# A long convolution by Fourier stages beside a feed-forward: the spectra buffers K and U turned from [frequency, channel] to [channel, frequency], and the ranks of the tasks set anew

## The chip, the core and the metric

The kernel runs on one core of a Trainium2 chip. The metric is device time in microseconds of one execution; less is better. A core has a matrix engine (PE, with a separate row PEld for its weight loads), three engines for elementwise work (DVE, ACT, POOL), and SP, whose queue issues the DMAs. On-chip memory is SBUF and, for matmul results, PSUM; both have 128 partitions.

## What is computed

```
x = A_u                                        # [1, 2048, 640] float32
g = sigmoid((x * gate_w).sum(-1))              # one gate per position
# state-space convolution: a kernel K[d, l] of 2048 taps for each of 640 channels
dt = exp(log_dt);  A = -exp(log_A_real) + 1j * A_imag
C  = (C_real + 1j * C_imag) * dt[:, None]
K  = 2 * einsum("dn,dnl->dl", C, exp((A * dt[:, None])[:, :, None] * arange(L))).real
a  = irfft(rfft(K, 2L) * rfft(u^T, 2L), 2L)[:, :, :L]^T + u * D_skip
b  = relu(x @ w1) @ w2                         # 640 -> 1728 -> 640
out = g * a + (1 - g) * b
```

## The kernel before

Three strands of work share the engines.

- **Feed-forward** (`feed_forward`): three passes over parts of the 1728 hidden columns (5, 5 and 4 tiles of 128), eight groups of 256 positions in each. Operands are split into a high and a low part, and three products stand for one. In the views its matmuls write the tile `pf`; `pf<-xx,w1…` is the first layer and `pf<-w2…` the second. It has few dependencies on the rest and fills PE wherever the other strands wait.
- **Generation of the taps** (`params`, `ssm`): decay rates to phases and magnitudes (ACT with sine and exponential tables, DVE with products), then small matmuls into `pk`, a DVE transpose into `kt`, and a store of the taps to DRAM (`kd`).
- **The convolution** (`conv`), for five blocks `i` of 128 channels. A 2048-point transform is made of two stages of small matmuls. All of its matmul results go through a ring of three PSUM tiles named `pc`, and its spectra live in an SBUF tile `ku` with a half K for the taps and a half U for the signal, two such tiles for the five blocks. A half holds, on each partition, 32 frequencies (or time residues) by 128 channels, with the channels innermost: `[128, 32, C]`. The steps of one block are:
  1. `stage1`, four tasks for taps (source `ck`) and four for the signal (source `xu`): matmuls with the table `tf` into `pc`, and for each task two DVE transposes of 32 by 32 blocks (`turn`) from `pc` into K or U: 16 transposes.
  2. `stage2`, eight tasks `j`: 16 matmuls with the table `tm` whose moving operand is one frequency of K and of U, `st['ku', i][r, :, g]`, 256 columns; then an ACT copy of one half of the result into K (`ku<-pc`), two DVE products (`kx<-pc,ku` and, in place, `ku<-pc,ku`) and two POOL additions (`ku<-ku,kx`). `whole(i, j)` is the part of K that they share. This is the complex product of the two spectra.
  3. `inv2`, two halves: 64 matmuls each with `tn`, moving operand `whole(...)[r, q, p]` of 128 columns, then two ACT copies back into U (`back`, 128x1024).
  4. `relay`, eight DVE transposes from U into K (`ku<-ku`).
  5. `inv1`, four tasks: matmuls with `tw`, moving operand four time residues of K, 512 columns, then ACT multiplies by the gate into `yo`, and the results are joined with the feed-forward's and stored.

The program lists a float32 matmul once and the trace shows it as two instructions: 640 of the program with `tm` are 1280 in the trace.

The order is decided while the kernel is built. Each piece of work is a task (`Plan.add`) with an engine, a queue, a duration in us, dependencies, and a rank; `Plan.run` walks through time by these durations and takes on each engine the ready task of lowest rank, then issues it. On the chip every engine runs its instructions in that order. The rank of task number `n` is the one in its `add` plus `MOVES.get(n, 0)`; `MOVES` is a dictionary with one entry of ±0.7, ±1.5 or ±3 for some hundreds of the more than 2400 tasks. `relay` has a variant by DMA (`RL`), which is not in use. Lines of the profile are mostly L346, the helper through which all instructions are issued, so groups are told apart by tile names.

Of the kernel before, what the change touches and what calls it, by code (L numbers as in the profile page):

```python
# [60 lines left out]
RL = 'dve'  # L61
# [64 lines left out]
class Ring:  # L126
# [8 lines left out]
MOVES = {  # L135
# [59 lines left out]
}  # L195


class Task:
    __slots__ = ('eng', 'q', 'dur', 'fn', 'deps', 'take', 'use', 'prio', 'mode', 'lag', 'end', 'kb', 'glue', 'port', 'n', 'late')


class Plan:

# [164 lines left out]
class Kernel:  # L368
# [850 lines left out]
    def conv(self, C=128):  # L1219
# [49 lines left out]
        self.late_loads.append(tf)  # L1269
        K, first, pes = {}, {}, {}  # L1270


        def stage1(kind, i, q, src):
            s_, ld = src
            b_ = tok('psc')
# [267 lines left out]
```

## Time and profile before

| | |
|---|---|
| runs | 656.8, 662.4 and 1206.32 us; median 662.4 us |
| profiled execution | span 659.1 us; the page gives no other time of it, and what lies around the span is not shown |
| PE | 627.4 us busy (95%), 8236 matmuls |
| DVE | 550.5 us busy (84%), 778 instructions |
| ACT | 401.8 us busy (61%) |
| POOL | 93.5 us busy (14%) |
| mean granted clock of PE | 0.991 |

The share of busy time is a mean over strands with different limits. The generation of taps lies at about 85 to 395 us and the convolution at about 400 to 645 us of the span; feed-forward matmuls lie between them from start to end. A busy PE is not PE at its peak, since matmuls overlap. A row of a group reads: line, engine, operation, output from inputs, shapes, count, then busy time in us, the mean length of one in ns, and the idle time before them with what ended it. A row of the table by stretches gives start and end in us, length, busy time of each engine with the count of instructions, then the granted PE clock, the share of the DMA engines and GB/s.

### The profile page before, as it was taken

The page shows a single profiled execution, that of the slowest core. Times are in us where ns is not written, and L with a number is a line of the kernel's source. Part 1 is how long each engine was busy: PE and PEld are TensorE (multiplying, and loading weights), DVE is VectorE, ACT ScalarE, POOL GpSimd, SP SyncE. Part 2 cuts the span into 40 slices and gives each one's busy share as a digit, 9 for nine tenths or more (in the row PEclk, how much of TensorE's full clock was granted, in tenths as well). Part 3 has the DMA queues.
Part 4 walks back from the last instruction along what each step waited for, and adds up shares of the span by engine and source line. Part 5 has one row for each costly group of instructions (what it writes and reads, how often), then busy time and mean ns, then how long its engine had stood idle before and what let it go on. Part 6 is the DMA issues. An engine that isn't in the chain of part 4 may idle for free. (4 is left out here: it accounts for less than half of the span.)

```text
span 659.1 us, 19189 instructions
## 1 busy us (share of the span) xinstructions
PE 627.4 (95%) x8236; PEld 505.4 (77%) x8236; DVE 550.5 (84%) x778; ACT 401.8 (61%) x603; POOL 93.5 (14%) x133
## 2 busy tenths in 40 slices
PE   7999989999999999999999999998999999879896
PEld 7999989898987988998898995755666446735576
DVE  4899859999999899898999976894999778888552
ACT  5476389999998988979889821222431533334521
POOL 0000000000000000000000000240600622424541
PEclk9999999999999999999999999999999999989999
DMA  9963854143445532542424159946056756363526
GB/s 265 318 220 145 239 189 152 59 153 131 131 133 178 206 129 75 186 148 77 178 97 139 56 174 260 274 153 141 3 198 205 192 145 154 108 184 75 159 64 144
DMA packets 76303, 102.79 MB, mean 156 GB/s; under 512 B 7610, under 2 KB 59450, under 8 KB 75963
## 3 DMA queue, kind: packets, MB, share of 16 engines
q1 hardware_dynamic: 76058, 101.16, 51.0%
q8 instruction: 65, 1.06, 0.7%
q10 hardware_dynamic: 160, 0.41, 0.2%
q14 instruction: 20, 0.16, 0.1%
HBM read 62.36 MB, written 39.19 MB: 154 GB/s over the span
## 5 line engine op out<-in xcount | busy, mean ns | idle before, releaser
L346 PE MATMUL pf<-xx,w1h 128*128 128x256 f32 (+1 forms) x760 | 185.5, 341 | 0.8 <-ACT q L346 0.4
L346 PEld LDWEIGHTS pf<-xx,w1h 128*128 128x128 f32 x760 | 124.8, 190 | 30.6 <-issue 16.2
L346 PE MATMUL pf<-xx,w1l 128*128 128x512 f32 (+1 forms) x340 | 116.0, 341 | 3.0 <-issue 3.0
L346 PE MATMUL pf<-w2h,hh 128*128 128x320 f32 x288 | 89.2, 314 | 0.1
L346 PE MATMUL pf<-w2l,hh 128*128 128x320 f32 x288 | 87.8, 309 | 0.0
L346 ACT COPY ku<-pc 128x512 f32<-128x512 f32 (+1 forms) x60 | 42.8, 732 | 71.2 <-PE pc L346 71.0
L346 DVE STREAM_TRANSPOSE ku<-pc 128x512 f32<-128x512 f32 x80 | 76.4, 1051 | 10.1 <-PE pc L346 10.0
L346 PE MATMUL pf<-w2h,hl 128*128 128x320 f32 x256 | 74.0, 315 | 0.0
L346 PEld LDWEIGHTS pf<-xx,w1l 128*128 128x128 f32 x340 | 64.5, 190 | 7.7 <-DVE w1l L346 0.2
L346 POOL TENSOR_TENSOR ku<-ku,kx 128x256 f32<-128x256 f32 x80 | 55.9, 734 | 81.1 <-PE pf L346 31.0
L346 POOL TENSOR_TENSOR kt<-kt,dsk 128x8 f32<-128x8 f32 x20 | 10.3, 516 | 382.0 <-DVE kt L346 370.8
L346 DVE TENSOR_TENSOR sc<-pg,sc 128x1024 f32<-128x1024 f32 x40 | 48.7, 1217 | 12.1 <-ACT sc L346 11.9
L346 PEld LDWEIGHTS pf<-w2h,hh 128*128 128x128 f32 x288 | 54.1, 188 | 4.9 <-issue 2.4
L346 DVE STREAM_TRANSPOSE ku<-ku 128x512 f32<-128x512 f32 x40 | 46.9, 1237 | 10.7 <-ACT ku L346 8.6
L346 PEld LDWEIGHTS pf<-w2l,hh 128*128 128x128 f32 x288 | 54.1, 188 | 0.8
L346 ACT ACT_TABLE_LOAD x42 | 53.9, 1283 | 0.8
L346 ACT CAST sc<-pg 128x1024 int32<-128x1024 f32 x40 | 40.5, 1012 | 19.0 <-PE pg L346 18.7
L346 PEld LDWEIGHTS pf<-w2h,hl 128*128 128x128 f32 x256 | 46.2, 188 | 7.5 <-issue 7.1
L346 DVE TENSOR_TENSOR mg<-mg,sc 128x1024 f32<-128x1024 f32 x40 | 48.9, 1223 | 1.8
L346 DVE TENSOR_TENSOR sc<-sc,me 128x1024 f32<-128x1024 f32 x40 | 48.6, 1216 | 0.0
L346 ACT ACTIVATE yo<-pc,gate 128x128 f32<-128x128 f32 x78 | 22.1, 373 | 39.3 <-DMA out_dram<-yo 18.7
L346 ACT ACTIVATE sc<-sc,half_pi 128x1024 f32<-128x1024 f32 x40 | 45.6, 1139 | 0.0
(168 smaller groups left out, 1255.2 us busy)
## 6 DMA issues: line engine op xcount, KB each, us to landing
xx<-xt SPq DMA_DIRECT2D x24, 640.0 KB, 5.3
xt<-xx SPq DMA_DIRECT2D x16, 640.0 KB, 6.6
part<-q SPq DMA_DIRECT2D x16, 640.0 KB, 2.9
q<-part SPq DMA_DIRECT2D x16, 640.0 KB, 4.8
ws<-in_B_w_dram SPq DMA_DIRECT2D x20, 320.0 KB, 5.2
kd<-kt SPq DMA_DIRECT2D x80, 64.0 KB, 1.7
ck<-kd SPq DMA_DIRECT2D x40, 128.0 KB, 2.9
xu<-in_A_u_dram SPq DMA_DIRECT2D x10, 512.0 KB, 7.5
```

The lines of the kernel that those rows point to most:

```text
L346: return lambda *a, **k: self._tc.keep_in_program_order(f(*a, **k))
```

## The change

K and U keep their size, but the 128 channels become the outer and the 32 frequencies the inner index: a helper view `(e g f)` with `f=1` puts 32 frequencies of one channel next to each other. The transposes of `stage1` and `relay` now write (and `relay` also reads) runs without gaps; everything that takes one frequency for all channels now steps by 32 elements, 128 bytes: the moving operands of `tm`, `tn` and `tw`, the outputs of the ACT copies, one input of both DVE products, the output of the one in place, and the POOL additions' `ku` operands. The tile `kx` stays as it was. The planner's duration of a `stage1` transpose goes from 1.0 to 0.68, that of a relay from 1.17 to 0.7; the other durations stay. `MOVES` is replaced as a whole: a function `moves()` gives ranks to families of tasks, among them many tasks outside the convolution. The numbers of instructions by engine, and of DMAs, do not change. The order does, on every engine.

```diff
-RL = 'dve'
...
-MOVES = {
-    2: 1.5, 21: -3, 26: 1.5, 31: -1.5, 48: 3, 52: -3, 62: -1.5, 75: -1.5, 76: -0.7, 84: -3, 94: -0.7, 108: 0.7,
...
+def moves():
+    r = {}
+    for v, s in (
+            (-3.11, "739-741"),
+            (-2.81, "2"),
...
+            (-2.19, "1341-1677/56 1732"),
...
+            (0.51, "1266-1281/5"),
...
+            (3.6, "1327"),
+    ):
+        for x in s.split():
+            a, _, step = x.partition('/')
+            a, _, b = a.partition('-')
+            for i in range(int(a), int(b or a) + 1, int(step or 1)):
+                r[i] = v
+    return r
+MOVES = moves()
...
+        def blocks(x, d0):
+            return x[:, :, d0:d0 + 16].rearrange("p g e f -> p e f g")
...
-                        st['ku', i] = self.pr.tile([128, 2, 32, C], F32, name="ku", bufs=2)
+                        t = self.pr.tile([128, 2, 32, C], F32, name="ku", bufs=2)
+                        st['ku', i] = t.rearrange("p k a b -> p k (a b)").rearrange("p k (e g f) -> p k g e f", g=32, f=1)
                         st['K', i], st['U', i] = st['ku', i][:, 0], st['ku', i][:, 1]
...
-                    V.transpose(out=st['K' if k else 'U', i][:, :, d].rearrange("p g d -> p d g"), in_=pv)
+                    V.transpose(out=blocks(st['K' if k else 'U', i], d0), in_=pv)
...
-            ts = [A('DVE', 's' + kind, 1.0, turn(h), [a], use=[b_, buf], rank=SKD if k else SUD)
+            ts = [A('DVE', 's' + kind, 0.68, turn(h), [a], use=[b_, buf], rank=SKD if k else SUD)
...
         def whole(i, j):
-            return st['K', i][:, 4 * j:4 * j + 4].rearrange("q (b p) c -> q b p c", b=2)
+            return st['K', i][:, 4 * j:4 * j + 4].rearrange("q (b p) e f -> q b p e f", b=2)
...
         def relay(i, r, dep):
...
-            d = slice(r * 16, r * 16 + 16)
-            return A('DVE', 'rl', 1.17, lambda: V.transpose(out=st['K', i][:, :, d].rearrange("p b d -> p d b"),
-                                                           in_=st['U', i][:, :, d].rearrange("p g d -> p d g")),
+            return A('DVE', 'rl', 0.7, lambda: V.transpose(out=blocks(st['K', i], r * 16), in_=blocks(st['U', i], r * 16)),
                      dep, use=[K[i]], rank=RLR)
```

In `stage2`, `inv2`, `back` and `inv1` only the views are spelled anew, with the two indices `e f` where `c` stood.

More of the change, by code (lines that the diff above doesn't have):

```diff
@@ L131, in token @@
         return Token(self)
-MOVES = {
[59 rows of a table removed]
-}
+def moves():
+    r = {}
+    for v, s in (
[111 rows of a table added]
+    ):
[6 more added lines that the diff above has]
+MOVES = moves()
 class Task:
@@ L1298, in go @@
                         pv, d0 = p.rearrange("p h (b d) -> p d h b", d=32)[:, 16 * h:16 * h + 16], q * 32 + h * 16
-                    d = slice(d0, d0 + 16)
-                    V.transpose(out=st['K' if k else 'U', i][:, :, d].rearrange("p g d -> p d g"), in_=pv)
+                    V.transpose(out=blocks(st['K' if k else 'U', i], d0), in_=pv)
                 return go
@@ L1324, in pe @@
                             r, g = slice(p * 64, p * 64 + 64), 4 * j + m
-                            self.E.matmul(ps[32 * m:32 * m + 32, p, 2 * a:2 * a + 2], st['tm'][r, g, 32 * a:32 * a + 32],
-                                          st['ku', i][r, :, g], start=True, stop=True)
-                st['p2', i, j] = ps.rearrange("q p (a k) c -> q k a p c", a=2)
+                            self.E.matmul(ps[32 * m:32 * m + 32, p, 2 * a:2 * a + 2].rearrange("q k (e f) -> q k e f", f=1),
+                                          st['tm'][r, g, 32 * a:32 * a + 32], st['ku', i][r, :, g], start=True, stop=True)
+                st['p2', i, j] = ps.rearrange("q p (a k) (e f) -> q k a p e f", a=2, f=1)
             def copy():
@@ L1335, in go @@
                     if a:
-                        st['kx', i, j] = self.pr.tile([128, 2, 2, C], F32, name="kx", bufs=KX)
-                    V.tensor_mul(st['kx', i, j] if a else k, st['p2', i, j][:, 1, None, a].to_broadcast([128, 2, 2, C]), k)
+                        st['kx', i, j] = self.pr.tile([128, 2, 2, C], F32, name="kx", bufs=KX).rearrange(
+                            "q b p (e f) -> q b p e f", f=1)
+                    V.tensor_mul(st['kx', i, j] if a else k,
+                                 st['p2', i, j][:, 1, None, a].to_broadcast([128, 2, 2, C, 1]), k)
                 return go
@@ L1367, in pe @@
                                 r = slice(32 * m, 32 * m + 32)
-                                self.E.matmul(px[m // 2][p * 64:p * 64 + 64, m % 2, g], st['tn'][r, 4 * h + g, p, q],
+                                self.E.matmul(px[m // 2][p * 64:p * 64 + 64, m % 2, g].rearrange("q (e f) -> q e f", f=1),
+                                              st['tn'][r, 4 * h + g, p, q],
                                               whole(i, 4 * h + g)[r, q, p], start=q == 0, stop=q == 1)
@@ L1372, in go @@
                 def go():
-                    S.copy(st['U', i][:, 16 * h:16 * h + 16].rearrange("q (g m) c -> q m g c", m=4)[:, 2 * k:2 * k + 2],
-                           st['p3', i, h][k])
+                    S.copy(st['U', i][:, 16 * h:16 * h + 16].rearrange("q (g m) e f -> q m g e f", m=4)[:, 2 * k:2 * k + 2],
+                           st['p3', i, h][k].rearrange("q m g (e f) -> q m g e f", f=1))
                 return go
@@ L1385, in relay @@
         def relay(i, r, dep):
-            x = slice(32 * r, 32 * r + 32)
-            if RL == 'dma':
-                return A('SP', 'rl', 0.62, lambda: D_.dma_start(st['K', i][x], st['U', i][x].rearrange("b g d -> g b d")), dep,
-                         use=[K[i]], kb=512, rank=2)
-            d = slice(r * 16, r * 16 + 16)
-            return A('DVE', 'rl', 1.17, lambda: V.transpose(out=st['K', i][:, :, d].rearrange("p b d -> p d b"),
-                                                           in_=st['U', i][:, :, d].rearrange("p g d -> p d g")),
+            return A('DVE', 'rl', 0.7, lambda: V.transpose(out=blocks(st['K', i], r * 16), in_=blocks(st['U', i], r * 16)),
                      dep, use=[K[i]], rank=RLR)
@@ L1411, in pe @@
                     for h in range(2):
-                        self.E.matmul(py[h * 64:h * 64 + 64, 0], st['tw'],
-                                      st['K', i][:, h * 16 + b0:h * 16 + b0 + 4, :], start=True, stop=True)
+                        self.E.matmul(py[h * 64:h * 64 + 64, 0].rearrange("q b (e f) -> q b e f", f=1), st['tw'],
+                                      st['K', i][:, h * 16 + b0:h * 16 + b0 + 4], start=True, stop=True)
                 def copy(q=q, b0=b0, ns=ns, y_=y_, first=first):
@@ L1493, in conv @@
                     new += stage1('k', i + 1, q, load_k(i + 1, q))
-            rl = [relay(i, r, xs) for r in range(4 if RL == 'dma' else 8)]
+            rl = [relay(i, r, xs) for r in range(8)]
             if more:
```

164 rows, old and new, of tables (MOVES, r) are left out of this document.

## The prediction

> **What bounds the kernel now.** I read the page first: the span, the busy times, the chain by line.
>
> ```profile
> span 659.1 us, 19189 instructions
> PE 627.4 (95%) x8236; PEld 505.4 (77%) x8236; DVE 550.5 (84%) x778; ACT 401.8 (61%) x603; POOL 93.5 (14%) x133
> PE pc L346 7%; PE pf L346 6%; DVE ku L346 3%; POOL ku L346 1%; SPq L346 1%; DMA out_dram<-yo 0%; ACT yo L346 0%; ACT ku L346 0%; DVE q L346 0%; ACT q L346 0%; DVE kx L346 0%; POOLq L1539 0%; DVEq L346 0%; ACTq L346 0%; DMA xu<-part 0%
> ```
>
> PE is busy for 95% of the span, so a faster DVE pays only where PE waits for it. The chain holds the transposes into `ku` with 3%. Next I read the table by stretches of ten microseconds over the convolution (start, end, length, busy time of PE, PEld, DVE, ACT, POOL, then the granted clock).
>
> ```profile
> 450.00:460.00 10.00, 7.51 (x289) 5.71 (x295) 2.17 (x3) 3.38 (x5) 0.00 (x0) 0.96 0.91 194
> ...
> 500.00:510.00 10.00, 10.00 (x72) 6.43 (x71) 9.29 (x12) 0.46 (x1) 0.73 (x1) 1.00 0.73 207
> ...
> 560.00:570.00 10.00, 8.35 (x245) 6.50 (x245) 8.18 (x12) 3.29 (x5) 7.16 (x11) 1.00 0.37 142
> 570.00:580.00 10.00, 10.00 (x165) 6.99 (x146) 10.00 (x12) 4.44 (x11) 1.62 (x2) 1.00 0.30 90
> 580.00:590.00 10.00, 6.66 (x51) 3.19 (x53) 10.00 (x11) 3.84 (x10) 1.66 (x2) 0.95 0.68 189
> 590.00:600.00 10.00, 9.57 (x50) 3.37 (x47) 7.83 (x11) 1.14 (x4) 3.22 (x3) 0.71 0.50 140
> ...
> 620.00:630.00 10.00, 7.32 (x134) 6.04 (x119) 3.89 (x5) 4.08 (x5) 1.30 (x1) 1.00 0.66 194
> ...
> 650.00:659.00 9.00, 3.04 (x21) 2.77 (x19) 1.21 (x3) 0.00 (x0) 1.60 (x3) 0.90 0.58 139
> sum 264.00, PE 243.64 PEld 155.06 DVE 197.54 ACT 84.89 POOL 82.32; mean PE 9.37 PEld 5.96 DVE 7.60 ACT 3.26 POOL 3.17
> ```
>
> From 395 us on PE is idle for 264 - 243.6 = 20.4 us. Between 500 and 510 DVE is nearly full and PE too: feed-forward matmuls cover the transposes. Between 560 and 600 they don't: DVE stands at 10.0 of 10, PE loses 1.65 + 0 + 3.34 + 0.43 = 5.4 us, and the clock falls to 0.95 and 0.71, another (0.05 + 0.29) x 10 = 3.4 us of work: 8.8 us in all. The chain in order of time (start, length, what) says which work that is.
>
> ```profile
> 566.72 3.01 DVE ku L346 x3
> ...
> 570.13 3.41 DVE ku L346 x3
> ...
> 573.94 0.99 DVE ku L346
> ...
> 575.44 14.14 DVE ku L346 x14
> ...
> 624.89 12.61 PE pf L346 x60
> ...
> 637.60 3.65 PE pc L346 x16
> 641.26 4.76 PE pf L346 x31
> ```
>
> The first four pieces are 21.6 us of DVE on the path that sets the end, 21 instructions, all transposes but one product, about 1.03 us each: the relays of one block and transposes of `stage1` for the next, one after the other. The last relays, before 637, are not on the chain: 60 feed-forward matmuls stand over them.
>
> **The change part by part.** The costs of the tiles that are turned, by the view of groups with shapes kept apart:
>
> ```profile
> L346 DVE STREAM_TRANSPOSE ku<-pc 128x512 f32<-128x512 f32 x80 | 76.4, 1051 | 10.1 <-PE pc L346 10.0
> L346 DVE STREAM_TRANSPOSE ku<-ku 128x512 f32<-128x512 f32 x40 | 46.9, 1237 | 10.7 <-ACT ku L346 8.6 <-issue 2.1
> L346 DVE TENSOR_TENSOR ku<-pc,ku 128x512 f32<-128x512 f32 x40 | 27.6, 691 | 1.3
> L346 DVE TENSOR_TENSOR kx<-pc,ku 128x512 f32<-128x512 f32 x40 | 27.3, 683 | 10.3 <-ACT ku L346 9.5 <-POOL ku L346 0.6
> L346 DVE STREAM_TRANSPOSE kt<-pk 128x512 f32<-128x512 f32 x20 | 14.3, 713 | 8.7 <-PE pk L346 6.5 <-issue 2.2
> L346 ACT COPY ku<-pc 128x512 f32<-128x512 f32 x40 | 23.5, 587 | 39.8 <-PE pc L346 39.6
> L346 ACT COPY ku<-pc 128x1024 f32<-128x1024 f32 x20 | 19.3, 1021 | 31.4 <-PE pc L346 31.4
> L346 POOL TENSOR_TENSOR ku<-ku,kx 128x256 f32<-128x256 f32 x80 | 55.9, 734 | 81.1 <-PE pf L346 31.0 <-PE pc L346 25.3 <-DVE ku L346 24.7
> L346 PE MATMUL pc<-ku,tm 64*32 64x256 f32 x1280 | 42.5, 386 | 2.8 <-issue 1.8 <-DVE ku L346 0.5 <-PE pc L346 0.2
> L346 PE MATMUL pc<-ku,tn 32*64 32x128 f32 x1280 | 22.2, 274 | 2.9 <-issue 2.9
> L346 PE MATMUL pc<-ku,tw 128*64 128x512 f32 x80 | 19.5, 607 | 1.6 <-ACT yo L346 1.0 <-DVE ku L346 0.4
> ```
>
> *The 120 transposes.* The kernel has the same operation without steps: `kt<-pk`, same size, 713 ns. One that writes with a step of 512 bytes takes 1051, one that reads and writes so 1237. The change takes both kinds to runs without gaps, so I price them at 713: 338 ns less for each of 80, 524 ns for each of 40, together 27 + 21 = 48 us of DVE. The lower bound of the saving is nothing (the `kt` transposes run in another stretch, where something else might favour them). On the path of 566 to 590 the 20 transposes save 6.8 us if all were of the cheap kind and 10.5 if all were relays; what PE loses there, 8.8 us, lies between, and I take that. What is late next there is PE with its own feed-forward work, which was waiting.
>
> *What now steps by 128 bytes.* No row shows an elementwise operation or a matmul with such a step on its main operand, so I bound them. Below: nothing, and a gain is excluded, since the operand is only spread. Above, by the transposes: a stepped read adds 1237 - 1051 = 186 ns to 512 elements, read and write 524. That makes 0.19 us for each `kx` product and 0.52 for each in place, 40 x 0.71 = 28 us of DVE; up to 0.34 us for a short ACT copy and 0.68 for a long one, 40 x 0.34 + 20 x 0.68 = 27 us on ACT, which is busy for 85 of 264 us; and on PE 0.36 ns for each column read. For POOL there is a nearer row, the additions on `kt`, 8 elements at this very step:
>
> ```profile
> L346 POOL TENSOR_TENSOR kt<-kt,dsk x20: 209/567/704, 111.1 to 393.6; 128x8 f32<-128x8 f32 x20
> ...
> L346 POOL TENSOR_TENSOR q<-q,ku 128x128 f32<-128x128 f32 x2 | 0.9, 462 | 3.1 <-DVE q L346 3.1
> ```
>
> 128 elements take 462 ns and 256 take 734, that is 2.1 ns each over a start of 190; eight should take 207, and the shortest took 209. So POOL pays nothing by its row, and that is the nearest row in engine and step. For PE the pass of 512 columns takes 607 ns and that of 256 386, 0.86 ns per column, and several of these matmuls run at once on the same partitions (1280 x 386 ns, 494 us, fit into 42.5 us). I take nothing for all four, because the transposes differ from them in the step as well (512 bytes) and move blocks; the upper ends go into the rivals and the range.
>
> The Trainium skill speaks against the change here: "Advanced Engine Details and Errata", section "Memory Cachelines", says that SBUF has lines of 16 bytes, that two accesses at least have to fall into a line to hide its latency, and that a new line for every access costs. A step of 128 bytes is a new line for every element as 512 was. The two slow rows of transposes agree with it; no row shows it for PE, ACT or products, and it gives no price. By it the third rival below comes true.
>
> *The ranks.* The numbers of instructions and DMAs are the same on every engine; the orders differ from the first microseconds on. By the orders of the two built programs, 1833 feed-forward matmuls stand ahead of the convolution's first matmul before and 1896 after (15 more of the first layer, 48 of the second), and 79 and 96 stand behind its last. By the chain's rows a matmul of the first layer takes about 12.61 / 60 = 0.21 us and one of the second 4.76 / 31 = 0.15, so 10.5 us of cover go from the convolution to the generation before it. On SP's queue the load of the gate weights goes ahead of six weight loads, and stores and loads of the convolution change places with those of `part`, `q` and `xx`. What waits for DMAs and instructions now:
>
> ```profile
> ACT yo L346 <- DMA out_dram<-yo: 18.7, 7, 7.2
> ...
> PE pc L346 <- issue: 5.5, 5, 2.5
> ...
> PE pc L346 <- DMA xu<-in_A_u_dram: 0.6, 1, 0.6
> ```
>
> Of DMAs PE itself waits 0.6 us here; ACT's 18.7 us are covered by its 61%. The idle time in 450 to 460 and 620 to 630, 2.5 and 2.7 us, is mostly "issue", in which no engine is late; I leave it. Ahead of the convolution the bounds are these stretches:
>
> ```profile
> 50.00:100.00 50.00, 46.71 (x346) 44.84 (x346) 38.55 (x74) 32.35 (x61) 0.00 (x0) 1.00 0.58 186
> 100.00:150.00 50.00, 48.39 (x675) 45.42 (x675) 48.96 (x69) 47.56 (x65) 1.55 (x3) 1.00 0.36 120
> ```
>
> PE idles 3.3 + 1.6 = 4.9 us there, the most that other ranks can give back; the most that they take is the 10.5 us of cover, if the convolution misses it. I count them as zero.
>
> *The sum.* Of the 20.4 us of idle PE, 6.0 are the tail after 650, 5.4 the stretch 560 to 600, 5.2 the two "issue" stretches; 3.8 remain in small waits for results of DVE, ACT and POOL. With 48 us less on DVE I count these as gone too. 659.1 - 8.8 - 3.8 = 646.5 us. I take the span as the profiled execution's time; it lies between the two ordinary runs, 656.8 and 662.4, and 0.5% below the median.
>
> **The rivals.**
>
> 1. *The products give the relief back.* If a step costs a product what it costs a transpose, a block saves 16 x 0.338 + 8 x 0.524 = 9.6 us and pays 8 x 0.71 = 5.7. Of the 12.6 us gained 41% stay: 659.1 - 5.2 = 653.9 us. For it: the same engine and memory. Against it: another operation, a quarter of the step.
> 2. *The transposes were hidden anyway.* At 500 to 510 DVE is as full and PE loses nothing; if the new order of work covers 560 to 600 with or without the shorter transposes, or opens another hole, the time stays at about 659.
> 3. *PE reads slower (the other side).* The matmuls with `tm`, `tn` and `tw` are busy for 42.5 + 22.2 + 19.5 = 84.2 us on the engine that bounds everything. With 0.36 ns on 0.86 per column they grow by 42%, 35 us: 646.5 + 35 = 682 us. Above 15% (12.6 / 84.2) the gain is gone. For it: several matmuls read the same partitions at once, each column then from another place. Against it: the first layer reads up to 512 columns in 0.21 us, 0.41 ns each, so 0.86 leaves every read about twice that time.
> 4. *The change doesn't do what it says.* If the transposes into `ku` are slow for another reason than their step (PSUM shared with PE, say), they stay at about 1.05 us, and the new order, with 10.5 us less cover, lacks it: 659.1 + 10.5 = 669.6 us.
>
> **How the numbers follow.** A measurement of this kernel can tell about 2% from no change; that is 649.2 and 675.6 us around the median. Forecast 0.47, of which 0.38 lie below 649.2 and 0.09 above; rival 1 0.15 (0.02 faster, 0.11 within, 0.02 slower, where ACT's copies grow too); rival 2 0.10, all within; rival 3 0.22 (0.19 slower); rival 4 0.06 (0.02 slower). Faster 0.40, within 0.37, slower 0.23. The forecast's own range is 640 to 653: below, the 4.9 us before the convolution; above, half of the gain. The whole range, 637 to 676, takes in rivals 1, 2 and 4 and the milder half of rival 3 and leaves out 0.04 below and 0.16 above.
>
> **What would show it.** Right: transposes `ku<-pc` and `ku<-ku` both at 700 to 760 ns; DVE busy near 500 us; products at 690, ACT copies at 590 and 1020, POOL additions at 735; busy time of the three matmul groups within 3 us of 84.2; no stretch of the convolution with DVE at 10.0 and PE under 8, and no clock under 0.9 there. Wrong: a matmul with `tm` well over 386 ns (rival 3), products over 850 ns (rival 1), transposes near 1050 (rival 4), or all rows as forecast and the span at 659 (rival 2).

## The result, and the profile after

The changed kernel takes 759.28 us (median of 4 runs, 758.47 to 759.43) against 660.74 us: 1.1497 times as long, 95% interval 1.1457 to 1.1538. Ratios and intervals, here and below, leave out two slow runs of the kernel before, 1206.32 and 667.41 us. The profiled execution took 758.47 us with a span of 756.7, so about 1.8 us lie around the span. The prediction, 646.5 us with a whole range of 637 to 676, was wrong in sign, and the result lies far above the third rival too, 682.

First the page after: span, busy times, and the shares of the engines in the chain of work that ended last.

```profile
span 756.7 us, 19202 instructions
PE 734.5 (97%) x8236; PEld 528.6 (70%) x8236; DVE 542.4 (72%) x778; ACT 437.1 (58%) x603; POOL 107.1 (14%) x133
PE 73%; ACT 10%; DVE 9%; DMA 3%; issue 3%; SPq 1%; POOL 0%; POOLq 0%; DVEq 0%; ACTq 0%
```

PE is busy for 107 us longer with the same 8236 matmuls; the span is 97.6 us longer. DVE is 8 us shorter, not 48. The groups on the turned tiles, shapes kept apart, in the order in which they were priced:

```profile
L408 DVE STREAM_TRANSPOSE ku<-pc 128x512 f32<-128x512 f32 x80 | 50.7, 684 | 32.4 <-PE pc L408 32.2
L408 DVE STREAM_TRANSPOSE ku<-ku 128x512 f32<-128x512 f32 x40 | 25.5, 691 | 22.8 <-ACT ku L408 14.3 <-POOL q L408 5.7 <-issue 2.8
L408 DVE TENSOR_TENSOR ku<-pc,ku 128x512 f32<-128x512 f32 x40 | 46.7, 1166 | 1.2
L408 DVE TENSOR_TENSOR kx<-pc,ku 128x512 f32<-128x512 f32 x40 | 40.9, 1023 | 56.5 <-ACT ku L408 55.0 <-POOL ku L408 1.4
L408 ACT COPY ku<-pc 128x512 f32<-128x512 f32 x40 | 41.7, 1042 | 105.5 <-PE pc L408 105.5
L408 ACT COPY ku<-pc 128x1024 f32<-128x1024 f32 x20 | 37.4, 1971 | 36.2 <-PE pc L408 36.2
L408 POOL TENSOR_TENSOR ku<-ku,kx 128x256 f32<-128x256 f32 x80 | 69.9, 901 | 126.7 <-DVE ku L408 94.5 <-PE pc L408 27.9 <-PE pf L408 4.2
L408 PE MATMUL pc<-ku,tm 64*32 64x256 f32 x1280 | 113.8, 876 | 2.6 <-DVE ku L408 2.6
L408 PE MATMUL pc<-ku,tn 32*64 32x128 f32 x1280 | 43.2, 417 | 1.9 <-ACT ku L408 1.6 <-issue 0.3
L408 PE MATMUL pc<-ku,tw 128*64 128x512 f32 x80 | 37.1, 1040 | 3.7 <-ACT yo L408 3.1 <-DVE ku L408 0.6
```

Everything that now steps by 128 bytes has become slower, on all four engines, and only the transposes have become faster. The three matmul groups grew from 84.2 to 194.1 us of busy time, 110 us. Of what they read and write only the moving operands lie differently. One half of `inv2` shows it in the timeline, before and after (start, length):

```profile
619.48 2.07 PE L346 MATMUL pc<-ku,tn 32*64 32x128 f32 x126 [0.43 <-issue]
```

```profile
588.36 4.29 PE L408 MATMUL pc<-ku,tn 32*64 32x128 f32 x128
```

The same work (the first row lacks two of the 128, which stand just before it) takes 4.29 instead of 2.07 us, with no other matmul between. In most stretches of the convolution PE has few holes left; two of them, and the sum:

```profile
480.00:500.00 20.00, 20.00 (x222) 7.01 (x222) 14.96 (x15) 7.30 (x8) 9.20 (x11) 1.00 0.36 133
...
620.00:640.00 20.00, 20.00 (x254) 7.13 (x243) 11.34 (x11) 7.44 (x13) 10.64 (x12) 1.00 0.07 18
...
sum 362.00, PE 345.50 PEld 174.41 DVE 191.13 ACT 116.81 POOL 96.84; mean PE 19.19 PEld 9.69 DVE 10.62 ACT 6.49 POOL 5.38
```

PE is idle for 16.5 of 362 us from 395 us on (20.4 of 264 before), and the clock stands at 1.00 in all stretches but 540 to 560 (0.91) and the last (0.94). PEld, the weight loads, is busy for about a third of the two stretches shown, and for 48% of the whole (59% before): PE is full, but each matmul takes longer.

### The profile page after: what moved, and what is told of

Read it like the earlier page. It is cut to its first block, busy times and chain, and to the rows that moved or that the text cites. A ratio compares the mean times of both kernels' runs of the same rounds, so it can differ in the third digit from the quotient of the medians.

```text
span 756.7 us, 19202 instructions
## 1 busy us (share of the span) xinstructions
PE 734.5 (97%) x8236; PEld 528.6 (70%) x8236; DVE 542.4 (72%) x778; ACT 437.1 (58%) x603; POOL 107.1 (14%) x133
## 4 chain that ended last, share of the span: by engine, by line
PE 73%; ACT 10%; DVE 9%; DMA 3%; issue 3%; SPq 1%; POOL 0%; POOLq 0%; DVEq 0%; ACTq 0%
PE pf L408 37%; PE pc L408 27%; PE pk L408 5%; ACT sc L408 2%; ACT ku L408 2%; DVE sc L408 2%; PE pg L408 2%; PE px L408 2%; SPq L408 1%; ACT L408 1%; DVE G L408 1%; DVE ku L408 1%; DVE mg L408 1%; ACT mg L408 1%; DVE hl L408 1%
## 5 line engine op out<-in xcount | busy, mean ns | idle before, releaser
L408 ACT COPY ku<-pc 128x512 f32<-128x512 f32 (+1 forms) x60 | 78.9, 1352 | 141.7 <-PE pc L408 141.7
L408 PE MATMUL pc<-ku,tm 64*32 64x256 f32 x1280 | 113.8, 876 | 2.6 <-DVE ku L408 2.6
L408 POOL TENSOR_TENSOR ku<-ku,kx 128x256 f32<-128x256 f32 x80 | 69.9, 901 | 126.7 <-DVE ku L408 94.5
L408 DVE TENSOR_TENSOR kx<-pc,ku 128x512 f32<-128x512 f32 x40 | 40.9, 1023 | 56.5 <-ACT ku L408 55.0
L408 PEld LDWEIGHTS pc<-ku,tm 64*32 64x32 f32 x1280 | 30.8, 136 | 66.6 <-issue 65.2
L408 DVE STREAM_TRANSPOSE ku<-pc 128x512 f32<-128x512 f32 x80 | 50.7, 684 | 32.4 <-PE pc L408 32.2
L408 ACT ACTIVATE hh<-pf 128x512 fp32r<-128x512 f32 (+1 forms) x40 | 20.4, 510 | 55.7 <-PE pf L408 55.6
```

What stands on the lines that cost most here:

```text
L408: return lambda *a, **k: self._tc.keep_in_program_order(f(*a, **k))
```

## The experiments

Three theories: (1) PE: the stepped reads of the matmuls; (2) the elementwise chain of `stage2`, whose links grew too; (3) the new order. Each comparison is with the kernel before on the same chip; its median was 660.7 to 661.8 us.

### The two halves of the change apart

`layout_only` is the changed kernel with the old ranks and durations, `ranks_only` the kernel before with the new ones. On every engine the first runs in the order of the kernel before, the second in the order of the changed one.

```diff
 # layout_only: open layout of the change
-MOVES = moves()                         +MOVES = { ...the old dictionary... }
-A('DVE', 's' + kind, 0.68, ...)         +A('DVE', 's' + kind, 1.0, ...)
-A('DVE', 'rl', 0.7, ...)                +A('DVE', 'rl', 1.17, ...)
 # ranks_only: the old layout, these three lines the other way round
```

> The new layout of K and U with the old ranks and the old planner durations, so that every engine runs its instructions in the order of the kernel before. Three theories. (1) PE: the loss is the time that matmuls with tm, tn and tw take on operands with a step of 128 bytes; then nearly all of it stays here: 745 to 775 us, the three groups near 114, 43 and 37 us busy as in the changed kernel. (2) Elementwise chain: the loss is the longer copies, products and additions of stage2; also 745 to 775 here. (3) Ranks: the loss comes from the new order, planned with durations that are too short; then 650 to 675 here.

> The old layout with the new ranks and the new planner durations, in the order of the changed kernel. Theories 1 and 2: 655 to 670 us; transposes back at 1.05 and 1.24 us, and the order has 10.5 us less feed-forward cover in the convolution, so at most 670. Theory 3 (ranks): 720 to 760.

Measured: `layout_only` 757.43 us, 1.1481 (1.1423 to 1.1538); `ranks_only` 675.89 us, 1.0244 (1.019 to 1.0298). The layout alone makes the whole loss, so theory 3 falls as its cause. But the ranks are not neutral: on the old layout they cost 15 us, more than the 670 us allowed for; by the interval this is between 1.9 and 3.0%. The groups of `ranks_only`:

```profile
L409 DVE STREAM_TRANSPOSE ku<-ku 128x512 f32<-128x512 f32 x40 | 46.1, 1214 | 10.6 <-issue 8.9 <-ACT ku L409 1.7
...
L409 PE MATMUL pc<-ku,tw 128*64 128x512 f32 x80 | 23.0, 678 | 10.5 <-DVE ku L409 9.6 <-ACT yo L409 0.8
```

PE waits 9.6 us for long relays ahead of `tw`, where the kernel before waits 0.4: the order was planned for relays of 0.70 us. The rest of the 15 us was not traced; the granted clock, 0.984 to 0.990 in these runs and 0.991 to 0.998 in those of the kernel before that they are compared with, may hold a part of it.

### Two runs with more waits than meant

`pe_flat` let the matmuls of the changed kernel read runs without gaps at other places of the same tile, `pe_step` let those of the kernel before step through the tile. Both read other numbers of the tile.

```diff
 # pe_flat, raw is the tile of the change seen as [128, 2, 32, C]
-st['ku', i][r, :, g]                    +st['raw', i][r, :, g]
-whole(i, 4 * h + g)[r, q, p]            +st['raw', i][r, 0, 4 * (4 * h + g) + 2 * q + p]
 # pe_step: the reverse, in the kernel before
```

> The changed kernel, but the moving operands of tm, tn and tw are runs without gaps at the same place in the same tile (so the matmuls get other numbers of the same tile); transposes, copies, products and additions stay in the new layout. Theory 1 (PE): the three groups fall from 194 to about 85 us and the span by about as much, to 645 to 670 us. Theory 2 (elementwise): the groups fall but the chain still holds: over 710. Theory 3: over 710 too.

> The kernel before, but the moving operands of tm, tn and tw step by 128 bytes through the same tile (other numbers of it); all else in the old layout and order. Theory 1 (PE): groups near 114, 43 and 37 us, 750 to 780 us. Theory 2 and 3: the matmuls' time is covered, 660 to 690.

Measured: 738.63 us, 1.1175 (1.111 to 1.124), and 802.01 us, 1.2157 (1.2097 to 1.2217). Neither answers the question. A flat run in the new layout covers four channels of all frequencies, and so elements that the products of other tasks `j` write; the matmuls wait for them. The waits of PE in `pe_flat` from 400 us on, and the group `tm` of `pe_step`:

```profile
PE pc L408 <- POOL ku L408: 24.7, 15, 2.9
PE pc L408 <- DVE ku L408: 23.5, 15, 2.7
PE pc L408 <- ACT ku L408: 12.9, 14, 1.3
```

```profile
L346 PE MATMUL pc<-ku,tm 64*32 64x256 f32 x1280 | 117.1, 872 | 29.8 <-POOL ku L346 24.2 <-ACT ku L346 4.2 <-DVE ku L346 1.5
```

What they do show is that the duration of `tm` goes with the step of its read in either layout: 872 ns in the old one with the step, 500 in `pe_flat` (with waits inside, and at a clock of 0.93). The next runs take the step away, or put it in, without touching an element more.

### PE alone, elementwise alone, both

The rows of K and U in the old layout hold 128 channels without gaps. Reading them in a permuted sequence puts 128 bytes between one column and the next (after every fourth it goes back, to the neighbour of the first) and touches the same elements. `pe_perm` does so for the matmuls, `ele_perm` for copies, products and additions, `both_perm` for both, `ele_act` for the copies alone. The columns of their results are permuted.

```diff
 # pe_perm (a=4: channels 0, 32, 64, 96, 1, ...; pe_perm32 has a=32: 0, 4, 8, ...)
-st['ku', i][r, :, g]
+st['ku', i][r, :, g].rearrange("q k (a c) -> q k c a", a=4)
 # ele_perm
-S.copy(whole(i, j), st['p2', i, j][:, 0])
+S.copy(perm(whole(i, j)), flat(st['p2', i, j][:, 0]))     # and so in products, additions, back
 # perm: "q b p (a c) -> q b p c a", a=4;  flat: "q b p (c a) -> q b p c a", a=4
```

> The kernel before; the moving operands of tm, tn and tw are the same rows of K and U with their 128 channels read in another sequence (0, 32, 64, 96, 1, 33, ...), so that each column lies 128 bytes from the last and no matmul touches an element that it didn't touch before (the result's columns come out permuted). Theory 1 (PE): the loss is there: groups near 114, 43 and 37 us busy, 745 to 775 us. Theory 2 (elementwise chain): 660 to 690.

> The kernel before; the ACT copies, both DVE products and the POOL additions go through the rows of K and U in that permuted sequence (128 bytes apart), with the same elements touched; matmuls and transposes as before (columns of the result come out permuted). Theory 1 (PE): the longer copies (about 1.04 and 1.98 us), products (1.02 and 1.15) and additions (0.90) are mostly covered: 660 to 685 us. Theory 2: 720 to 760.

> The kernel before with the permuted reads of PE (alone +55 us) and the permuted copies, products and additions (alone +30). If both sit on one path, one behind the other: about 745 us. If PE's longer work covers the longer elementwise chain: 715 to 728.

> The kernel before with only the ACT copies permuted (1.1 and 2.0 us); products and additions as before. All three kinds together cost 30 us. If the copies, first in the chain of stage2 and holding the pc tiles, carry it: 680 to 692. If the products on DVE carry it: 660 to 670.

Measured: `pe_perm` 716.59 us, 1.0827 (1.0802 to 1.0852); `ele_perm` 691.85, 1.0455 (1.0431 to 1.048); `both_perm` 724.05, 1.0955 (1.0922 to 1.0987); `ele_act` 669.42, 1.0131 (1.0092 to 1.017). The matmul groups of `pe_perm`:

```profile
L346 PE MATMUL pc<-ku,tm 64*32 64x256 f32 x1280 | 76.6, 620 | 0.0
L346 PE MATMUL pc<-ku,tn 32*64 32x128 f32 x1280 | 39.2, 401 | 0.0
...
L346 PE MATMUL pc<-ku,tw 128*64 128x512 f32 x80 | 37.1, 1057 | 2.3 <-DVE ku L346 1.3 <-ACT yo L346 0.9
```

They grow by 68.7 us, the kernel by 55: theory 1 holds in kind, though less than I expected, because `tm` takes 620 ns here and 876 in the changed kernel. From `ele_perm`:

```profile
L346 ACT COPY ku<-pc 128x512 f32<-128x512 f32 x40 | 42.1, 1109 | 42.0 <-PE pc L346 42.0
L346 DVE TENSOR_TENSOR kx<-pc,ku 128x512 f32<-128x512 f32 x40 | 43.4, 1086 | 8.7 <-ACT ku L346 8.7
L346 PE MATMUL pc<-ku,tm 64*32 64x256 f32 x1280 | 43.2, 386 | 19.9 <-DVE ku L346 18.9 <-ACT ku L346 1.0
```

PE now waits 18.9 us for products ahead of `tm`. So theory 2 is no rival but a second cost, 30 us when it stands alone, above the 660 to 685 that theory 1 allowed. The copies alone cost 8; the rest appears only with products and additions, which were not tried by themselves. With matmuls and elementwise operations both permuted, the kernel grows by 63 us and not by 55 + 30 = 85: 22 us of the longer chain are covered by a PE that is busy longer, and PE waits for DVE 4.6 us in place of 29.5:

```profile
PE pc L346 <- DVE ku L346: 29.5, 32, 2.0
```

```profile
PE pc L346 <- DVE ku L346: 4.6, 4, 1.9
```

(the waits of PE from 395 us on, `ele_perm` first, then `both_perm`).

### The same from the side of the changed kernel

`pe_same` lets all three matmul groups read channel 127 of their frequency for every column, a step of nothing; channel 127 is written by the last transpose of each kind, so the waits stay. `tm_same` does so for `tm` only. All columns of a result then hold one channel's values.

```diff
-st['ku', i][r, :, g]
+st['ku', i][r, :, g, C - 1:].to_broadcast([64, 2, C, 1])
 # pe_same: tn and tw likewise
```

> The changed kernel; tm, tn and tw read channel 127 of their frequency for all 128 columns (a step of nothing; the result has one channel's values in all columns), so that PE has no stepped reads and still waits for the last transpose of a block. Elementwise operations stay stepped. Theory 1 (PE): groups near 85 us in sum, 650 to 680 us. Theory 2: over 715.

> The changed kernel where only tm reads channel 127 for all columns; tn and tw stay stepped. All three flat gave 687 us, all stepped 759. tm's group is 68 of the 102 us by which the groups grow; if each group counts by its growth: about 711 us. If tm alone decides: 690 to 700. If tn and tw do: over 735.

Measured: `pe_same` 687.38 us, 1.039 (1.0361 to 1.0419); `tm_same` 713.26, 1.0773 (1.0737 to 1.0809). So 72 of the 98.5 us go with the matmuls' reads, 46 of them with `tm`'s and 26 with those of `tn` and `tw`, each near its share of the busy time (the groups are 68, 18 and 16 us shorter in `pe_same`). `pe_same` stays above the 680 expected, and PE waits for the elementwise chain in it:

```profile
L408 PE MATMUL pc<-ku,tm 64*32 64x256 f32 x1280 | 45.4, 407 | 16.6 <-DVE ku L408 13.0 <-ACT ku L408 1.2 <-ACT w2h L408 1.2
...
L408 DVE TENSOR_TENSOR ku<-pc,ku 128x512 f32<-128x512 f32 x40 | 46.3, 1157 | 1.2
```

### Why `tm` suffers most

In the changed kernel the frequencies `g` = 4j to 4j + 3, which four `tm` matmuls read at once on the same partitions, are neighbouring floats; in `pe_perm` they lie 512 bytes apart. But `pe_perm` also comes back to a line (16 bytes, four floats, as in the prediction) after four columns. `pe_perm32` keeps the streams apart and comes back after 32; its columns lie 16 bytes apart.

> As pe_perm, with the channels read 4 apart (0, 4, 8, ..., 124, 1, 5, ...): 16 bytes between columns, the same line again only after 32 columns, and the four streams of tm 512 bytes apart as in pe_perm. In pe_perm tm took 620 ns (the same line again after 4 columns), in the changed kernel 876 (its four streams then read neighbouring floats of one line). If the closeness of the streams makes the difference: tm near 620 again, about 715 us. If the quick return to a line made pe_perm cheaper: tm near 870, 745 to 760 us.

Measured: 717.36 us, 1.0847 (1.0817 to 1.0876), and

```profile
L346 PE MATMUL pc<-ku,tm 64*32 64x256 f32 x1280 | 77.0, 629 | 0.0
```

as in `pe_perm`. The quick return is not what made it cheaper. That leaves the closeness of the four streams as the likely reason: in `pe_step` they read neighbouring floats in the old layout, and `tm` took 872 ns. The two streams of `tw`, which are not neighbours in either, cost the same in both (1057 ns in `pe_perm`, 1040 in the changed kernel), and the two of `tn`, neighbours only in the changed kernel, nearly so (401 and 417). The same four streams apart in the new layout were not tried, so this stays an argument.

### The premise alone, and other lengths of run

`trans_runs` is the kernel before with transposes that go through the same elements with 16 channels next to each other; nothing else steps. `trans_runs_new` adds the new ranks. `runs_4` and `runs_2` are the new layout with `f=4` and `f=2`, old ranks; `runs_2_new` has the new ranks. The first two put numbers at other places, the last three compute all of the reference.

```diff
 # trans_runs
-V.transpose(out=st[...][:, :, d].rearrange("p g d -> p d g"), in_=pv)
+V.transpose(out=st[...][:, :, d], in_=pv)                      # relay: both sides
 # runs_4
-t.rearrange("p k a b -> p k (a b)").rearrange("p k (e g f) -> p k g e f", g=32, f=1)
+t.rearrange("p k a b -> p k (a b)").rearrange("p k (e g f) -> p k g e f", g=32, f=4)
```

> The kernel before; the transposes of stage1 and relay go through the same elements of K and U in the other sequence, 16 channels of one frequency next to each other (64-byte runs), so that only their length changes and their numbers land permuted. It is the premise of the prediction alone: short transposes, nothing else. If the prediction's sum was right: transposes near 0.7 us and 644 to 652 us. If short transposes are hidden (rival 2): 656 to 664.

> As trans_runs, with the new ranks and planner durations: the order of the changed kernel, which was planned for transposes of 0.68 and 0.70 us, with those and no stepped access. If the new order is good once its durations hold: 640 to 652 us. If it is worse by itself: 658 to 680, like the new ranks with long transposes (676).

> The new layout with runs of four channels (16 bytes) between the steps, f=4 instead of f=1, in the order and with the ranks of the kernel before. If a run of 16 bytes is enough for a full-rate read: matmul groups 84 to 95 us, copies and products as before; transposes write with a step of 16 bytes, between 0.69 and 1.05 us. With cheap transposes 645 to 655 us, with dear ones 657 to 665. If any step costs: matmul groups over 110 us and over 690.

> The new layout with runs of two channels (8 bytes), order and ranks of the kernel before. Runs of four leave everything at the old speed, transposes included (1.09 and 1.12 us). If two accesses to a line of 16 bytes are enough: matmul groups near 84 us, copies 0.59, products 0.69, and transposes between 0.69 and 1.05; 645 to 656 us. If not: groups 90 to 150 us and 665 to 720.

> Runs of two channels (short transposes, matmul groups 96 instead of 84 us, all correct) with the new ranks and durations, whose order gained 10 us with short transposes alone. If the 12 us of matmuls add to that: 660 to 664 us. If part of them is covered: 650 to 658, better than the kernel before.

| kernel | us | ratio to before | interval |
|---|---|---|---|
| `trans_runs` | 657.55 | 0.9952 | 0.992 to 0.9984 |
| `trans_runs_new` | 650.67 | 0.9854 | 0.9815 to 0.9892 |
| `runs_4` | 657.12 | 0.9934 | 0.9891 to 0.9978 |
| `runs_2` | 662.06 | 1.0023 | 0.9994 to 1.0052 |
| `runs_2_new` | 659.04 | 0.9966 | 0.9945 to 0.9986 |

All five lie within 2% of the kernel before. Short transposes alone, 691 and 684 ns, give 3 us and not 12.6. The stretch that was to give 8.8, in `trans_runs`, and a later one:

```profile
560.00:570.00 10.00, 9.94 (x297) 7.51 (x303) 9.29 (x16) 4.28 (x6) 8.35 (x13) 1.00 0.52 205
570.00:580.00 10.00, 9.93 (x142) 6.75 (x126) 6.26 (x11) 4.10 (x10) 1.76 (x2) 1.00 0.31 96
580.00:590.00 10.00, 7.93 (x62) 3.29 (x64) 6.32 (x10) 3.83 (x10) 1.47 (x2) 1.00 0.70 191
590.00:600.00 10.00, 8.38 (x65) 3.83 (x65) 6.60 (x11) 2.80 (x10) 4.27 (x4) 1.00 0.61 157
...
620.00:630.00 10.00, 6.84 (x25) 5.53 (x25) 3.13 (x6) 2.48 (x4) 2.78 (x3) 0.83 0.46 127
...
sum 264.00, PE 242.64 PEld 155.10 DVE 155.96 ACT 85.06 POOL 82.18; mean PE 9.33 PEld 5.97 DVE 6.00 ACT 3.27 POOL 3.16
```

From 560 to 600 the clock dips are gone and PE loses 3.8 us in place of 5.4, about 5 us in all. But 620 to 630 now has a dip to 0.83, where the kernel before stood at 1.00. DVE has 42 us of room, and PE's idle time in the whole convolution is 20.3 us as before (21.4 in the table, whose last stretch reaches 1.1 us past the end). The view of PE's waits from 395 us on says why, for the kernel before and then for `trans_runs`:

```profile
PE pc L346 <- DVE ku L346: 3.4, 5, 1.9
```

```profile
PE pf L346 <- issue: 4.0, 1, 4.0
PE pc L346 <- ACT yo L346: 4.0, 3, 1.7
PE pc L346 <- issue: 3.2, 2, 2.7
PE pc L346 <- DVE ku L346: 1.8, 4, 0.7
```

PE waited only 3.4 us for the writers of `ku` on DVE in the first place; 1.8 remain, and its waits for ACT's work on `yo` grow from 1.4 to 4.0. With the order planned for short transposes the gain is 10 us. The ranks are thus worth +15 us with long transposes and -7 with short ones, and about nothing where PE is slowed (759 against 757).

Runs of four leave the matmuls, copies, products and additions at their old speed, but the transposes stay long too. Runs of two make the transposes short, and the matmul groups 12 us longer. Group rows of `runs_4`, then of `runs_2`:

```profile
L345 PE MATMUL pc<-ku,tm 64*32 64x256 f32 x1280 | 41.5, 380 | 1.8 <-issue 1.0 <-DVE ku L345 0.4
...
L345 DVE STREAM_TRANSPOSE ku<-pc 128x512 f32<-128x512 f32 x80 | 78.7, 1087 | 8.6 <-PE pc L345 8.5
L345 DVE STREAM_TRANSPOSE ku<-ku 128x512 f32<-128x512 f32 x40 | 42.1, 1121 | 10.7 <-ACT ku L345 8.7 <-issue 2.1
```

```profile
L345 PE MATMUL pc<-ku,tm 64*32 64x256 f32 x1280 | 50.6, 451 | 0.0
L345 PE MATMUL pc<-ku,tn 32*64 32x128 f32 x1280 | 26.2, 309 | 2.0 <-issue 2.0
...
L345 DVE STREAM_TRANSPOSE ku<-pc 128x512 f32<-128x512 f32 x80 | 51.9, 693 | 21.9 <-PE pc L345 21.6
...
L345 ACT COPY ku<-pc 128x512 f32<-128x512 f32 x40 | 24.2, 604 | 44.1 <-PE pc L345 44.1
```

`runs_4` is 0.7% under the kernel before and `runs_2_new` 0.3%; both intervals end below 1, but neither difference has a cause shown, and single runs overlap (`runs_4` 654.8 to 661.6 us, the kernel before beside it 658.4 to 662.9). `runs_2` lies between its two expectations: the 12 us of matmuls cost 4.5 us against `trans_runs`, and 8 in the new order (`runs_2_new` against `trans_runs_new`).

## Why the prediction was wrong, by its own steps

- **The bound.** Right, and it should have ruled the rest: PE bounds the kernel, so an edit that lengthens PE's own work is paid for the most part. The 102 us by which the three groups are shorter in `pe_same` are worth 72 us of the kernel's time, the 69 us of `pe_perm` 55.
- **The 120 transposes.** The price was right: 684 and 691 ns for 713 forecast. What they are worth was not: alone they give 3 us (`trans_runs`), near rival 2, by which they were hidden anyway, and the sum's 12.6 is nearly reached, with 10, only by the ranks that belong to them. The chain and the idle time of a stretch showed where DVE came last, not what a shorter DVE would give: other waits ended soon after. The 3.4 us for dips of the granted clock were also counted as the transposes' loss, but a dip came back elsewhere. The 3.8 us of small waits, counted as gone, have no support in the run with the old order: PE's idle time in the convolution stayed at 20 us.
- **"What now steps by 128 bytes … I take nothing for all four."** This is the step that failed. All four grew, and on PE alone the groups by 110 us. Even the upper ends were too low for three of the four elementwise forms on DVE and ACT: the product in place grew by 475 ns (upper end 524), but `kx` by 340 (186), the short copy by 455 (340) and the long one by 950 (680). For POOL the nearest row misled: eight elements at 209 ns against 207 are too few to show a cost per element; with 256 the additions grew from 734 to 901.
- **Rival 3, the right mechanism, mis-sized.** Its price, 0.36 ns per column, came from transposes, one stream on another engine. Measured per column: `tw` 0.85 ns, (1040 - 607) / 512; `tn` 1.12, (417 - 274) / 128; `tm` 1.91, (876 - 386) / 256. That several matmuls read the same partitions at once was named and then left out of the price. The number of streams is not what sets it, though: with the streams apart, in `pe_perm`, the same sums give 0.88, 0.99 and 0.91, nearly alike for two streams (`tw`, `tn`) and four (`tm`). What doubles `tm` is likely that its four streams are neighbours. The argument against the rival, that 0.86 ns per column leave time for a read, failed for all three groups; no run has a single stream, so whether one alone would hide the step stays open.
- **Rival 1** was an addition and no alternative: products with copies and additions cost 30 us alone, 8 on top of PE's (`both_perm`); the products by themselves were not run. **Rival 4**, the new order with long transposes, was real in `ranks_only`: 15 us where 10.5 had been priced, 9.6 of them PE's wait for the relays; it doesn't bear on the changed kernel, whose transposes are short.
- **The rule of lines of 16 bytes.** The Trainium skill's "Memory Cachelines" ("Advanced Engine Details and Errata") was weighed and set aside; the runs bear it out. Four floats in a line cost nothing (`tm` 380 ns), one float costs on every engine. Its two accesses per line are nearly enough for the copies (604 against 587) and for `tw` (603 against 607), not for `tn` (309 against 274) and `tm` (451 against 386).

The account of the changed kernel, each step one run: 661 us before; -10 for short transposes with their ranks (650.7); +37 for the elementwise chain (`pe_same`, 687.4, whose matmul groups are still 7 us longer than those of the step before); +26 for `tn` and `tw` (`tm_same`, 713.3); +46 for `tm` (759.3). The shares hang on the order of the steps, because what comes later can be covered: with the matmuls first, the elementwise chain added only 8 us (`both_perm`).

## What to carry to other kernels

When a layout is turned so that one operation reads and writes without gaps, list every other operation on the tile with its new step, and price first those on the engine that bounds the kernel; that no row shows a cost does not make it nothing. Where no row has such an access, measure it alone or take the costlier end on the bounding engine, and look how close together the streams lie that read a partition at once. Before crediting a shorter operation, add up what the bounding engine waits for it. A run length between the extremes (here 8 and 16 bytes) shows which side pays, and ranks tuned for one set of durations belong to it: the same order was 15 us worse with long transposes and 7 better with short ones.

## What the runs showed of the hardware that was not expected

- For DVE's transposes of 128x512 float32 a step of the write costs only from somewhere between 8 and 16 bytes on: with 4, 8, 16 and 512 bytes they took 684, 693, 1087 and 1051 ns (the changed kernel, `runs_2`, `runs_4`, before).
- A matmul of 256 float32 columns (`tm`, four streams on the same partitions) takes 380 to 386 ns without a step. With one it takes 620 to 629 when the streams lie 512 bytes apart (`pe_perm` with 128 bytes between columns, `pe_perm32` with 16), and 872 to 877 when they read neighbouring floats (`pe_step`, the changed kernel, `layout_only`, 128 bytes).
- ACT's copies into rows with a step of 128 bytes take 1.78 and 1.93 times as long (587 to 1042 ns, 1021 to 1971 ns), POOL's additions 1.23 times (734 to 901).
